# Another listed order up to the fourth tile, the first batch's evictions shared between ScalarE and VectorE, and spare transposes on TensorE, in an attention and two-MoE kernel on one core

## The chip, the core and the metric
The kernel runs on one core of a Trainium2 chip. The metric is the device time of one execution in microseconds (us), given as the median of several runs; a profiled execution comes with a trace. TensorE (PE) multiplies, and its weight loads are listed as PEld; VectorE is DVE, ScalarE is ACT, GpSimd is POOL, and SyncE (SP) issues the DMAs. Each engine works through its own list of instructions in order and waits for the others by semaphores.

## What is computed
```python
def sm_attn(qq, kk, vv):                      # softmax attention, scale 1/8
    s = scale * np.matmul(qq, kk.transpose(0, 1, 3, 2))
    a = np.exp(s - np.max(s, axis=-1, keepdims=True))
    a = a / (np.sum(a, axis=-1, keepdims=True) + 1e-09)
    return np.matmul(a, vv)
p_packed = sm_attn(p, k, v)                   # 8 batches, 8 heads, 576 tokens, 64 wide, 32 packs
x = sm_attn(q, p_packed, p_packed)            # as 4608 tokens x 512
h = x @ w_in                                  # 512 -> 1024
solu = h * softmax(h)
ln = layernorm(solu) * g_ln
y = ln @ w_out                                # 1024 -> 512
h2 = np.maximum(np.maximum(y @ w1, y @ w2), y @ w3)   # 512 -> 768
out = h2 @ w_out2                             # 768 -> 512
```
The weights arrive as float64 and are decoded to float32 on the chip.

## The kernel before, in words
Three stages follow each other. The first, about the first 520 us, computes for each of 36 tiles of 128 tokens the attention and the hidden row `h`, turns its normalised row (`u`) and multiplies it by `w_out` in groups of four tiles (`y`). The second is the maximum of three products (line 957), the third the last product (line 1235).

In the first stage each batch has two groups of four heads. `keys` (line 389) turns the packs (`tp` to `pT`) and the keys (`tp` to `kT`, four copies a group) through TensorE; `scores` multiplies them and VectorE takes the maxima (line 416); `powers` is the exponential on ACT (line 425, `e`); `weights` turns `e` into `e1T`; `values` multiplies by the values (`pv`), and two scalings give `ppz` (line 463 on ACT in batch 0, line 465 on VectorE in the others); `turned_values` turns that to `ppT`. `queries` turns the queries into `qT` (lines 644, 651 in batches 0 and 1). `product` multiplies the packed values by `w_in` (`mp`, line 485), and ACT copies it as `Mh` (line 490); `product_low` is the rest `Ml` on VectorE (line 496). `tokens` is the second attention's scores and exponential (lines 527 to 539, `st`, `x`), `shares` its normalisation and the pair `ah`, `al` (lines 548 to 566). `hidden_parts` gives `h` from three matmuls for each of two groups (`Mh` with `ah`, `Ml` with `ah`, `Mh` with `al`, line 686), for a tile in two halves, then a maximum on VectorE (line 694), an exponential on ACT (696), a product on VectorE (701), a square (707) and a scaling (722) on ACT. `y_transpose` (769 to 776) and `y_product` (798) follow, with the pair `lh`, `ll`.

`w_in` comes in eight pieces, each decoded in three steps: two operations on ACT (lines 128, 129), two on VectorE (132, 135), one on POOL (140). `w_out` is decoded likewise in four pieces for the left half and in small ones after that, and split into `woh` and `wol` (lines 213, 214).

The function `ev` (line 300) sends an eviction of PSUM to ACT ('s') or VectorE ('v'), as the table `CFG` says: the string of the key is read at a running number.

The order of the opening is written out in `CFG['st']`, one word a step. Up to the bar all five engines keep that order; behind the bar, and for all later tiles, a scheduler places the steps by its own estimate, also between the fixed ones. The words: `k`, `v`, `q` load keys, values, queries of a group; `L` loads a piece of `w_in`; `G` and `g` load and scale the gains; `K`, `s`, `e`, `i`, `E`, `p`, `t`, `Q` are keys, scores, powers, inverses, weights, values, turned values, queries; `x` and `a` are tokens and shares of a part of the batch; `n`, `m` the product and its low half; `1`, `2`, `3` the three steps of the next `w_in` piece; `o` loads a piece of `w_out`, `4` to `7` are the steps of its decode; `H0a` is the first half of tile 0, `H0b` its second, `H0x`, `H0c`, `H0d` what follows on the other engines; a `b` ahead of a word is batch 1.

Of the kernel before, what the change touches and what calls it, by code (L numbers as in the profile page):

```python
# [13 lines left out]
AF = mybir.ActivationFunctionType  # L14
# [5 lines left out]
def f32(ap):  # L20
# [5 lines left out]
    kT='s',  # L26
    qT='s',
    e1T='s',
    ppT='sv',
    pTz='s',  # L30
    yt='sv',
    look=3,
    s1='DFNTAHTDTyATyDyTAFy',
    s2='DFNTAHTTyTyDyTAFy',
    s3='DFNTAHTWTyTyyTWFy',
    t1=9,
# [1 line left out]
    nf=2,  # L38
    nb=1,
    st=(  # L40
# [3 lines left out]
    ),  # L44
    s0='TyTyFTyNFTyDFHD',
# [15 lines left out]
def kernel(  # L61
# [15 lines left out]
    nc = tc.nc  # L77
    B, H, S, D = q.shape
# [5 lines left out]
    P = 128  # L84
    KP = 96
    KJ = S // KP
    HALF = S // 2
    NPAIR = H // 2
# [16 lines left out]
    ident = const.tile([P, P], F32, name="ident")  # L105
# [85 lines left out]
    def decode_w_in(c, n):  # L191
        ns = slice(n * 512, (n + 1) * 512)
        src, i = words(w_in)[c * P:(c + 1) * P, ns, :], 4 * n + c - 6
        if i < 0:
            raw = wide(src)
        else:
            raw = early[0].bitcast(I32)[:, i * DFF:(i + 1) * DFF].rearrange("r (f t) -> r f t", t=2)
            nc.sync.dma_start(out=raw, in_=src)
        t = lt_p.tile([P, TB], F32, tag="ll", name="dt")
        return [*decode(w_in_sb[:, c, ns], raw, t, parts=True)]  # L200
# [95 lines left out]
    def ev(key, out, in_, n=0):  # L296
        e = CFG[key]
        e = e[n % len(e)]
        if e == 's':
            nc.scalar.copy(out, in_)  # L300
        elif e == 'v':
            nc.vector.tensor_copy(out, in_)

    def bank(name):
        return ps_t.tile([P, 512], F32, tag="t", name=name)
# [16 lines left out]
    qT, ppT, Mh, Ml, A = {}, {}, {}, {}, {}  # L322
# [7 lines left out]
    class Packed:  # L330
# [58 lines left out]

        def keys(self, g):  # L390

            tp = bank("tp")
            nc.tensor.transpose(tp[:, :P], self.p[:, g, :, :].rearrange("r a d -> r (a d)"), ident)
            ev('pTz', pT, tp[:, :P])
            kT = self.kT[g] = self.room_kT(g)
            for hh in range(4):
                tp = bank("tp")
                for jj in range(3):
                    nc.tensor.transpose(
                        tp[:, jj * KP:(jj + 1) * KP], self.kt[g][:, hh, jj * P:(jj + 1) * P], ident[:KP, :KP]  # L400
                    )
                ev('kT', kT[hh], tp[:, :HALF], hh)

        def scores(self, g):
            s1 = [bank("s1") for _ in range(2)]
# [42 lines left out]
        def values(self, g):  # L448
            b = self.b
            pv = bank("pv")  # L450
            for j in range(KJ):
                jj = 2 * (j % 3) + j // 3
                for hh in range(4):
                    nc.tensor.matmul(
                        pv[NP * hh:NP * (hh + 1), :D],
                        lhsT=self.e1T[g][j // 3][:, j % 3, NP * hh:NP * (hh + 1)],
                        rhs=self.vt[g][:, hh, jj * D:(jj + 1) * D],
                        start=(j == 0), stop=(j == KJ - 1),
                    )
            ppz = self.room_ppz(g)  # L460
            for r in range(2):
                if b == 0:
                    nc.scalar.activation(ppz[:, r, :], pv[:, :D], AF.Copy, scale=self.rim[g][:, r:r + 1])
                else:
                    nc.vector.tensor_scalar_mul(ppz[:, r, :], pv[:, :D], self.rim[g][:, r:r + 1])
            self.ppz[g] = ppz

        def turned_values(self, g):
# [32 lines left out]
        def queries(self, c):  # L501
            b = self.b
            if c == 0:
                qT[b] = qt_p.tile([P, NPAIR, S], F32, tag="qT", name="qT")
            full, rest = S // P, S % P

            def turn(out, j):
                nc.tensor.transpose(out, self.qt[c][:, j, :, :].rearrange("r h d -> r (h d)"), ident)

            for i in range(2):  # L510
                tp = bank("tp")
                for j in range(full):
                    turn(tp[:, j * P:(j + 1) * P], full * i + j)
                ev('qT', qT[b][:, 2 * c + i, :full * P], tp, i)
            tp = bank("tp")
            turn(tp[:, :P], 2 * full)
            ev('qT', qT[b][:, 2 * c:2 * c + 2, full * P:], tp[:, :P].rearrange("r (i t) -> r i t", i=2))
# [66 lines left out]
    class First(Packed):  # L584
# [51 lines left out]
        def queries(self, n):  # L636
            b = self.b
            if n == 0:
                qT[b] = qt_p.tile([P, NPAIR, S], F32, tag="qT", name="qT")
            for j in range(2 * n, 2 * n + 2):  # L640
                t0 = j * P
                tp = bank("tp")
                for i in range(NPAIR):
                    nc.tensor.transpose(
                        tp[:, i * P:(i + 1) * P], self.qt[j][:, 2 * i:2 * i + 2, :].rearrange("r h d -> r (h d)"), ident
                    )
                ev('qT', qT[b][:, :, t0:t0 + P], tp.rearrange("r (i t) -> r i t", i=NPAIR), j)
            if n == 1:
                tp = bank("tp")
                for c in range(2):  # L650
                    nc.tensor.transpose(
                        tp[:, c * P:(c + 1) * P], self.tail[:, c].rearrange("r h d -> r (h d)"), ident
                    )
                ev('qT', qT[b][:, :, S - S % P:], tp[:, :2 * P].rearrange("r (i t) -> r i t", i=NPAIR))

    def parts_of(t):

# [123 lines left out]
    def open_y():  # L781
        first_h.close()
        return late.enter_context(tc.tile_pool(name="ps_y", bufs=1, space=PSUM, reuse_waits="tile"))
# [247 lines left out]
    def load_w_out():  # L1031
        if left:
            n = left.pop(0)
            raw = u_p.tile([P, DFF], F32, tag="u", name="raw").bitcast(I32)
            src = words(w_out)[2 * n * P:2 * (n + 1) * P, :HM, :]
            nc.sync.dma_start(
                out=raw.rearrange("r (k c) -> r k c", k=2), in_=src.rearrange("(k r) f t -> r k (f t)", r=P)
            )
            raws.append((n, raw.rearrange("r (f t) -> r f t", t=2)))

    def start_step(w):
        nonlocal woh, wol
        if w == 'W':
            woh, wol = (big.tile([P, KFF, DM], F32R, tag=x, name=x) for x in ("woh", "wol"))
        elif w == 'L':
            for d, f in zip(dec_i, decode_w_in(*pieces.pop(0))):
                d.append(f)
        elif w in '123':
            dec_i[int(w) - 1].pop(0)()
        elif w == 'G':  # L1050
            nc.sync.dma_start(out=g_sb, in_=g_ln.rearrange("(c r) -> r c", r=P))
        elif w == 'g':
            nc.gpsimd.tensor_scalar_mul(g_sb, g_sb, 0.125)
        elif w == 'o':
            load_w_out()
        elif w == 'Y':
            rooms.append(open_y())
        elif w == 'T':
            step_t(0, KFF)
        elif w == 'y':  # L1060
            step_y(0, 2 * KFF)
        elif w in '4567':
            if w == '4':
                for d, f in zip(dec_o, decode_w_out(*raws.pop(0))):
                    d.append(f)
            dec_o[int(w) - 4].pop(0)()
        elif w[0] == 'H':
            t = int(w[1])
            if t not in parts:
                parts[t] = hidden_parts(t)  # L1070
            parts[t][w[2]]()
        elif w[0] == 'b':
            second.run(w[1:])
        else:
            first.run(w)
# [44 lines left out]
    def step_t(j, most):  # L1120
        n = turned.get(j, 0)
        if j >= 0 and n < min(most, KFF):
            y_transpose(j, n)
            turned[j] = n + 1

    with tc.manual_schedule(engines={ENGINES[e] for e in CFG['fix']}):
        for w in CFG['st'].split('|')[0].split():
            start_step(w)
    for w in CFG['st'].split('|')[1].split():
        start_step(w)  # L1130
# [10 lines left out]
    for t in range(4, nt):  # L1141
        j, i = t // 4 - 1, t % 4
# [61 lines left out]
    j = NB - 1  # L1204
# [140 lines left out]
```

## Time and profile before
| | |
|---|---|
| median of 3 runs | 1100.88 us (1099.74 to 1102.63) |
| profiled execution | 1099.66 us |
| its span | 1097.9 us |
| instructions in it | 17988 |
| TensorE busy | 1040.2 us, 95% |
| VectorE, ScalarE, GpSimd busy | 678.0, 504.8, 268.3 us |
| granted clock of TensorE, mean | 0.992 |

The span is the time from the first to the last instruction of the profiled execution; its own time adds what lies around it. Busy time counts an engine's instructions, and an engine that is not busy waits for another, for a DMA, or has nothing to do.

### The profile page before, as it was taken

Reading aid. Unit: us, or ns where it says so; the run is one execution under the profiler, and the core shown is the slowest. Engines: PE = TensorE matmul, PEld = TensorE weight load, DVE = VectorE, ACT = ScalarE, POOL = GpSimd, SP = SyncE. Lnnn points to the kernel's source line nnn. Section 1 sums busy time; section 2 is a strip of 40 time slices with the busy share of each in tenths; the row PEclk is TensorE's granted clock in tenths of the full one; section 3 lists DMA queues with packets and bytes.
Section 4 is the critical chain, followed back from the end, with each engine's and each line's share of the span. In section 5 each row is a group of like instructions: output and inputs, shape, how many; then the busy total and the mean of one; then the engine's idle time right before and its main releaser. Section 6 shows DMA issues by size and latency. Waiting matters only on the chain.

```text
span 1097.9 us, 17988 instructions
## 1 busy us (share of the span) xinstructions
PE 1040.2 (95%) x6548; PEld 874.3 (80%) x6548; DVE 678.0 (62%) x1318; ACT 504.8 (46%) x993; POOL 268.3 (24%) x293
## 2 busy tenths in 40 slices
PE   6668999999999999999999999999999999999997
PEld 4255767677675777777899999999989999999995
DVE  1858767777867685664898736725745663672560
ACT  4577867776786756566333421321231132132112
POOL 0413312121211200041576610320140042031002
PEclk9979999999999999999999999999999999999999
DMA  9723545556365623146564644444444453443411
GB/s 280 159 79 108 151 135 155 163 146 186 100 189 143 180 63 84 59 129 204 186 218 158 220 143 116 140 158 124 142 148 144 125 183 115 118 122 119 122 48 58
DMA packets 139463, 154.27 MB, mean 141 GB/s; under 512 B 51824, under 2 KB 92272, under 8 KB 139376
## 3 DMA queue, kind: packets, MB, share of 16 engines
q1 hardware_dynamic: 139376, 153.14, 47.6%
q8 instruction: 52, 0.85, 0.3%
q14 instruction: 35, 0.29, 0.1%
HBM read 116.92 MB, written 36.18 MB: 139 GB/s over the span
## 4 chain that ended last, share of the span: by engine, by line
PE 50%; DVE 2%; issue 1%; DMA 1%; POOL 1%; ACT 1%; DVEq 0%; ACTq 0%; POOLq 0%
PE m L957 32%; PE o L1235 12%; PE y L798 4%; PE h L686 1%; DVE wt L857 1%; DMA out_dram<-ob 1%; DVE r L965 0%; PE tp L769 0%; DVE kept L965 0%; POOL w2l L830 0%; DMA wt<-wodram 0%; DMA wt<-wdram 0%; ACT ob L1244 0%; ACT u L722 0%; POOL hl L1021 0%
## 5 line engine op out<-in xcount | busy, mean ns | idle before, releaser
L798 PE MATMUL y<-lh,woh 128*128 128x512 f32 x288 | 118.1, 416 | 0.6 <-ACT lh L775 0.6
L798 PE MATMUL y<-ll,woh 128*128 128x512 f32 x288 | 115.4, 401 | 0.0
L798 PE MATMUL y<-lh,wol 128*128 128x512 f32 x288 | 114.5, 398 | 0.0
L990 ACT COPY q<-m 128x384 f32<-128x384 f32 x54 | 25.9, 479 | 178.4 <-PE m L957 178.4
L965 DVE TENSOR_TENSOR u<-m,q 128x384 f32<-128x384 f32 x54 | 30.0, 555 | 125.0 <-PE m L957 65.2
L1021 POOL TENSOR_TENSOR hl<-cur,hh 128x384 fp32r<-128x384 f32 x36 | 40.5, 1128 | 235.8 <-ACT hh L1020 235.8
L140 POOL TENSOR_TENSOR wt<-raw 128x256 int32<-128x256 int32 (+1 forms) x60 | 40.4, 674 | 193.1 <-DVE raw L135 80.2
L1235 PE MATMUL o<-w2h,hh 128*128 128x512 f32 x216 | 84.3, 390 | 1.4 <-ACT ob L1244 1.4
L1235 PE MATMUL o<-w2h,hl 128*128 128x512 f32 x216 | 84.8, 393 | 0.6 <-POOL hl L1021 0.6
L1235 PE MATMUL o<-w2l,hh 128*128 128x512 f32 x216 | 84.5, 391 | 0.0
L686 PE MATMUL h<-Mh,ah 128*128 128x512 f32 x160 | 67.8, 424 | 7.6 <-DVE u L701 4.8
L686 PE MATMUL h<-Ml,ah 128*128 128x512 f32 x160 | 66.1, 413 | 3.1 <-DVE Ml L496 3.1
L686 PE MATMUL h<-Mh,al 128*128 128x512 f32 x160 | 65.4, 409 | 0.0
L798 PEld LDWEIGHTS y<-lh,woh 128*128 128x128 f32 x288 | 53.9, 189 | 14.1 <-issue 1.9
L798 PEld LDWEIGHTS y<-lh,wol 128*128 128x128 f32 x288 | 54.2, 188 | 12.8 <-issue 0.8
L957 PE MATMUL m<-b22h,s 128*128 128x384 f32 x216 | 63.7, 335 | 0.0
L798 PEld LDWEIGHTS y<-ll,woh 128*128 128x128 f32 x288 | 54.5, 189 | 11.5 <-DVE ll L776 0.7
L957 PE MATMUL m<-t1h,s 128*128 128x384 f32 x216 | 63.7, 335 | 0.0
L957 PE MATMUL m<-t2h,s 128*128 128x384 f32 x216 | 63.6, 335 | 0.0
L957 PE MATMUL m<-t3h,s 128*128 128x384 f32 x216 | 63.6, 335 | 0.0
L965 DVE TENSOR_TENSOR kept<-r,kept 128x384 f32<-128x384 f32 x72 | 59.3, 823 | 2.4
L776 DVE SCALAR_TENSOR_TENSOR ll<-tp,g_sb,lh 128x512 fp32r<-128x512 f32 x72 | 52.1, 743 | 14.0 <-ACT lh L775 13.8
(206 smaller groups left out, 2714.8 us busy)
## 6 DMA issues: line engine op xcount, KB each, us to landing
s<-sdram SPq DMA_DIRECT2D x188, 256.0 KB, 2.9
kt<-in_k_dram SPq DMA_DIRECT2D x16, 576.0 KB, 5.2
ydram<-yt SPq DMA_DIRECT2D x36, 256.0 KB, 2.9
raw<-in_moe_w_dram SPq DMA_DIRECT2D x36, 256.0 KB, 3.1
b<-ydram SPq DMA_DIRECT2D x24, 384.0 KB, 4.6
out_dram<-ob SPq DMA_DIRECT2D x36, 256.0 KB, 2.6
vt<-in_v_dram SPq DMA_DIRECT2D x14, 576.0 KB, 4.8
sdram<-s SPq DMA_DIRECT2D x28, 256.0 KB, 2.1
```

Of the source, the lines that this page charges most:

```text
L140: nc.gpsimd.tensor_tensor(out=dst.bitcast(I32), in0=hi, in1=lo, op=ALU.add)
L686: nc.tensor.matmul(at['h'][:, n, :], lhsT=x, rhs=m[:, g, n * 512:(n + 1) * 512], start=(i == 0), stop=(i == len(ops()) - 1),)
L776: last[nc.vector] = nc.vector.scalar_tensor_tensor(out=ll, in0=tp, scalar=gc, in1=f32(lh), op0=ALU.mult, op1=ALU.subtract)
L798: nc.tensor.matmul(ys[half][m], lhsT=w[:, kc, ms], rhs=x, start=(kc == 0 and i == 0), stop=(kc == KFF - 1 and i == 2),)
L857: nc.vector.tensor_tensor(out=out, in0=x, in1=y, op=op)
L957: nc.tensor.matmul(out, lhsT=w, rhs=y, start=start and i == 0, stop=i == len(ops) - 1, skip_group_check=not start,)
L965: mark[0] = nc.vector.tensor_tensor(**what)
L990: mark[1] = nc.scalar.copy(q, ba)
L1021: nc.gpsimd.tensor_tensor(out=hl, in0=t, in1=f32(hh), op=ALU.subtract)
L1235: nc.tensor.matmul(ops[i], lhsT=x[:, ts], rhs=w, start=(c == 0 and n == 0), stop=(c == KF2 - 1 and n == 2),)
```

## The change
Seven edits. (1) The order up to the bar of `st` is another: `e0` stands ahead of `s1`; `Q0` stands between the two value steps; five first steps of the `w_in` decode are listed around `t0 t1`, two full decodes ahead of `x0`; `H1a` is ahead of `x1`; `m1` is ahead of `a1`; batch 1's `K0` and `s0` are ahead of `H0x`. (2) `w` is a new word: twelve transposes of the identity into a spare bank that nobody reads. It stands twice ahead of `n0` and once behind `bs0`. (3) In batch 0 the key copies follow 'svsvvvvv' over both groups (two on ACT, six on VectorE) and the query copies 'vvsvs'; later batches keep ACT. (4) `pT` goes to VectorE in all batches. (5) `ppT` of batch 0 goes to VectorE. (6) `ppz` of batch 0 goes to VectorE. (7) Nothing is added or taken away but the 36 spare transposes; the lists behind the bar differ in places, since the scheduler places them anew.

```diff
-    ppT='sv',
-    pTz='s',
+    ppT='v',
+    kT0='svsvvvvv',
+    qT0='vvsvs',
+    pTz='v',
...
-        ... K0 s0 K1 s1 e0 i0 E0 e1 i1 E1 p0 t0 p1 t1 Q0 1 2 3 1 x0 2 3 1 1 2 3 2 3 1 ... 1 a0 2 3 n0 1 m0 H0a ...
+        ... K0 s0 K1 e0 s1 i0 E0 e1 i1 E1 p0 Q0 p1 1 t0 t1 1 1 1 2 3 2 3 1 x0 2 3 2 3 1 1 w w n0 a0 1 2 3 m0 H0a ...
-        'n1 W a1 m1 H0b H1b bq0 bq1 H0x g 5 6 H1x H0c H1c H0d H2a H2b ...
+        'n1 W m1 a1 H0b H1b bq0 bq1 bK0 bv0 g H0x H1x 5 6 bs0 w H0c H1c H2a H2b ...
...
-                ev('kT', kT[hh], tp[:, :HALF], hh)
+                ev('kT' if b else 'kT0', kT[hh], tp[:, :HALF], 4 * g + hh)
...
-                if b == 0:
-                    nc.scalar.activation(ppz[:, r, :], pv[:, :D], AF.Copy, scale=self.rim[g][:, r:r + 1])
-                else:
-                    nc.vector.tensor_scalar_mul(ppz[:, r, :], pv[:, :D], self.rim[g][:, r:r + 1])
+                nc.vector.tensor_scalar_mul(ppz[:, r, :], pv[:, :D], self.rim[g][:, r:r + 1])
...
-                ev('qT', qT[b][:, :, t0:t0 + P], tp.rearrange("r (i t) -> r i t", i=NPAIR), j)
+                ev('qT' if b else 'qT0', qT[b][:, :, t0:t0 + P], tp.rearrange("r (i t) -> r i t", i=NPAIR), j)
...
+        elif w == 'w':
+            tp = bank("warm")
+            for i in range(12):
+                nc.tensor.transpose(tp[:, i % 4 * P:(i % 4 + 1) * P], ident, ident)
```

The list of ACT in the opening, from the second group's exponentials (`e1`) to the first decode of `w_in` (`dt`, `raw`), before (the numbers are those of the buffers):
```order
L425 ACTIVATE e1_274,se1_276<-s1_240,m1_250 128x288
L425 ACTIVATE e1_275,se1_276<-s1_241,m1_250 128x288
L300 COPY e1T_284<-tp_286 96x384
L300 COPY e1T_285<-tp_291 96x384
L463 ACTIVATE ppz_321<-pv_296,rim_261 128x64 x2
L300 COPY ppT_324<-tp_325 128x128
L463 ACTIVATE ppz_353<-pv_328,rim_282 128x64 x2
L300 COPY ppT_324<-tp_356 128x128
L300 COPY qT_359<-tp_360 128x4x128
L300 COPY qT_359<-tp_366 128x4x128
L128 ACTIVATE dt_145<-raw_143 128x512
L129 ACTIVATE raw_143<-raw_143,ulps_73 128x512
```
and now:
```order
L428 ACTIVATE e1_274,se1_276<-s1_244,m1_254 128x288
L428 ACTIVATE e1_275,se1_276<-s1_245,m1_254 128x288
L302 COPY e1T_284<-tp_286 96x384
L302 COPY e1T_285<-tp_291 96x384
L130 ACTIVATE dt_145<-raw_143 128x512
L131 ACTIVATE raw_143<-raw_143,ulps_73 128x512
L130 ACTIVATE dt_148<-raw_146 128x512
L131 ACTIVATE raw_146<-raw_146,ulps_73 128x512
```
The scalings, `ppT` and `qT` that stood between `e1T` and the first decode on ACT are on VectorE's list now.

The list of VectorE from the second part's scores (`st`) over the soft-max of `x` to the first maxima of `h` (`nm`) and the decode behind it, before:
```order
L533 STREAM_TRANSPOSE x<-st 128x320 x2
L537 TENSOR_REDUCE mx_508<-x 128x20
L538 TENSOR_TENSOR x<-x,mx_508 128x640
L548 TENSOR_REDUCE sm_533<-x 128x20
L549 TENSOR_SCALAR sm_533<-sm_533 128x20
L550 RECIPROCAL sm_533<-sm_533 128x20
L551 TENSOR_TENSOR x<-x,sm_533 128x640
L564 STREAM_TRANSPOSE y<-x 128x320 x2
L496 SCALAR_TENSOR_TENSOR Ml<-mp,Mh 128x512 x2
L694 TENSOR_REDUCE nm<-h 128x1
L132 TENSOR_SCALAR dt<-dt 128x512
L135 SCALAR_TENSOR_TENSOR raw<-raw,dt 128x512
```
and now:
```order
L533 STREAM_TRANSPOSE x<-st 128x320 x2
L537 TENSOR_REDUCE mx_541<-x 128x20
L538 TENSOR_TENSOR x<-x,mx_541 128x640
L496 SCALAR_TENSOR_TENSOR Ml<-mp,Mh 128x512 x2
L548 TENSOR_REDUCE sm_561<-x 128x20
L549 TENSOR_SCALAR sm_561<-sm_561 128x20
L550 RECIPROCAL sm_561<-sm_561 128x20
L551 TENSOR_TENSOR x<-x,sm_561 128x640
L564 STREAM_TRANSPOSE y<-x 128x320 x2
L304 COPY pT<-tp 128x128
L694 TENSOR_REDUCE nm<-h 128x1 x2
L134 TENSOR_SCALAR dt<-dt 128x512
```
`Ml` moved ahead of the sum and what follows it, `pT` of batch 1 came in ahead of the first maximum, and the two maxima follow each other; batch 1's score maxima stand behind that decode now.

The list of ACT from the last scalings of tiles 2 and 3 (`u`) to the first `lh`, before:
```order
L300 COPY pT<-tp 128x128
L300 COPY kT<-tp 128x288 x4
L707 ACTIVATE spare,squares<-u,nmu 128x1024
L722 ACTIVATE u<-u,nmu,powers 128x1024 x2
L425 ACTIVATE e_707,se_708<-s_688,m_698 128x288
L425 ACTIVATE e_707,se_708<-s_689,m_698 128x288
L213 CAST woh<-wt 128x2x256
L300 COPY e1T<-tp 96x384 x2
L775 ACTIVATE lh<-tp,g_sb 128x512 x2
```
and now:
```order
L707 ACTIVATE spare,squares<-u,nmu 128x1024
L722 ACTIVATE u<-u,nmu,powers 128x1024 x2
L215 CAST woh<-wt 128x2x256
L775 ACTIVATE lh<-tp,g_sb 128x512 x2
L302 COPY kT<-tp 128x288 x2
L130 ACTIVATE dt<-raw 128x512
```
The copies of batch 1's first keys, its exponentials and `e1T` stand further ahead on ACT's list now.

## Rows read from the trace of the kernel before
**Rows 1.** The page: busy time by engine, and TensorE's busy tenths in 40 slices.
```profile
PE 1040.2 (95%) x6548; PEld 874.3 (80%) x6548; DVE 678.0 (62%) x1318; ACT 504.8 (46%) x993; POOL 268.3 (24%) x293
...
PE   6668999999999999999999999999999999999997
```
**Rows 2.** By stretch: length, PE, PEld, DVE, ACT, POOL busy (count), PEclk, DMA share, GB/s.
```profile
85.02:120.00 34.98, 30.91 (x316) 20.25 (x315) 28.76 (x64) 25.49 (x61) 16.60 (x18) 1.00 0.43 117
120.00:140.00 20.00, 20.00 (x202) 15.57 (x204) 12.75 (x37) 18.45 (x39) 3.31 (x5) 1.00 0.60 154
```
**Rows 3.** Timeline of the opening: start, busy time, engine, line, operation, [idle before <-releaser].
```profile
23.96 1.92 PE L644 MATMUL tp<-ident,qu 128*128 128x128 f32 x8
...
27.09 0.43 DVE L132 TENSOR_SCALAR dt<-dt 128x512 int32<-128x512 int32 x1 [8.47 <-ACT dt L128]
...
34.91 3.64 PE L485 MATMUL mp<-w_in_sb,ppT 64*32 64x512 f32 x8 [0.32 <-POOL w_in_sb L140]
...
35.54 1.04 POOL L140 TENSOR_TENSOR w_in_sb<-raw 128x512 int32<-128x512 int32 x1 [0.68 <-issue]
...
41.70 1.04 PE L644 MATMUL tp<-ident,qu 128*128 128x128 f32 x8
...
47.41 1.05 PE L485 MATMUL mp<-w_in_sb,ppT 64*32 64x512 f32 x4 [0.25 <-POOL w_in_sb L140]
```
**Rows 4.** Loads of `raw`: SP's issue, time to landing (nine, 0:60).
```profile
7.68 7.61 SPq L188 DMA_DIRECT2D raw<-in_moe_w_in_dram  x6
...
DMA to landing us min/median/max: 3.4/7.4/10.5
```
**Rows 5.** Timeline from the second part's scores to the first maximum of `h`.
```profile
46.11 0.90 DVE L533 STREAM_TRANSPOSE x<-st 128x320 f32<-128x320 f32 x2
...
48.81 0.74 ACT L539 ACTIVATE x<-x 128x640 f32<-128x640 f32 x1 [3.81 <-DVE x L538]
...
49.45 1.06 ACT L490 ACTIVATE Mh<-mp 128x512 fp32r<-128x512 f32 x2
...
52.72 1.25 DVE L496 SCALAR_TENSOR_TENSOR Ml<-mp,Mh 128x512 fp32r<-128x512 f32 x2
...
53.42 0.80 PE L686 MATMUL h<-Ml,ah 128*128 128x512 f32 x1 [2.83 <-DVE Ml L496]
...
55.96 1.22 DVE L694 TENSOR_REDUCE nm<-h 128x1 f32<-128x1024 f32 x1 [2.00 <-PE h L686]
```
**Rows 6.** Tiles 2 and 3: TensorE's stretch alone, their first matmul, their last maximum.
```profile
60.60:66.40 5.80, 5.74 (x14) 0.50 0.25 85
...
60.66 0.77 PE L686 MATMUL h<-Mh,ah 128*128 128x512 f32 x1 [3.13 <-DVE u L701]
...
69.19 1.23 DVE L694 TENSOR_REDUCE nm<-h 128x1 f32<-128x1024 f32 x1 [1.36 <-PE h L686]
```
**Rows 7.** By stretch as rows 2, then the first `lh` and batch 1's second scores.
```profile
57.28:81.65 24.37, 15.52 (x73) 11.64 (x72) 13.92 (x37) 19.55 (x36) 4.91 (x6) 0.76 0.29 88
...
81.65 0.69 ACT L775 ACTIVATE lh<-tp,g_sb 128x512 fp32r<-128x512 f32 x1 [0.38 <-PE tp L769]
...
85.02 0.93 PE L408 MATMUL s<-kT,pT 64*32 64x288 f32 x16
```
**Rows 8.** Copies by shape (busy, mean ns); TensorE's waits for `pT`, 130:620 (total, times, longest).
```profile
L302 DVE COPY yt<-y 128x512 f32<-128x512 f32 x18 | 12.4, 688 | 4.9 <-PE y L798 4.8
L302 DVE COPY ppT<-tp 128x128 f32<-128x128 f32 x14 | 4.0, 289 | 5.2 <-PE tp L473 5.2
L300 ACT COPY kT<-tp 128x288 f32<-128x288 f32 x24 | 8.5, 407 | 4.0 <-PE tp L399 3.8
L425 ACT ACTIVATE e<-s,m 128x288 f32<-128x288 f32 x10 | 4.9, 495 | 0.0
L300 ACT COPY e1T<-tp 96x384 f32<-96x384 f32 x10 | 4.7, 486 | 2.1 <-PE tp L443 2.1
...
PE tp L399 <- ACT pT L300: 4.2, 5, 1.2
```

More of the change, by code (lines that the diff above doesn't have):

```diff
@@ L390, in keys @@
         def keys(self, g):
+            b = self.b
             tp = bank("tp")
@@ L653, in queries @@
                     )
-                ev('qT', qT[b][:, :, S - S % P:], tp[:, :2 * P].rearrange("r (i t) -> r i t", i=NPAIR))
+                ev('qT' if b else 'qT0', qT[b][:, :, S - S % P:], tp[:, :2 * P].rearrange("r (i t) -> r i t", i=NPAIR), 4)
     def parts_of(t):
```

4 rows, old and new, of the table st are left out of this document.

## The prediction
> **What bounds the kernel now.** I read the page first, then the busy time by stretch, then the timeline of the stretches in which TensorE idles, last the waits. The page shows TensorE busy for 95% of the span, with weak slices only at the front [rows 1]. By stretch it never stops between 120 and 140 us, and still misses 4.1 us between 85 and 120 [rows 2]. The change lists another order for the part before that, so the question is how much sooner the unbroken stretch begins: what is saved ahead of it comes off the end, since behind it little but TensorE is waited for.
>
> Four places set that front part. (a) VectorE starts the second half of the first `w_in` decode at 27.09, after 8.47 us of waiting for ACT's `dt`, though the six loads were issued from 7.68 on and landed at most 10.5 us after their issue [rows 3, 4]; ahead of ACT's decode stand evictions, in queue order. The fourth piece leaves POOL at 35.54 + 1.04 = 36.58, and the product `mp` ends at 34.91 + 3.64 = 38.55 [rows 3]. (b) From x1's transposes at 46.11 VectorE runs the whole soft-max of x1 before `Ml`, which starts at 52.72; TensorE waits 2.83 us for it, and the first maximum of `h` starts at 55.96 [rows 5]. (c) The halves of tiles 2 and 3 start at 60.66 after 3.13 us without work, and run at half the granted clock: 14 matmuls in 5.74 us, 0.41 us each [rows 6]. (d) From the first exponential to the first `lh` (57.28 to 81.65) ACT is busy 19.55 of 24.37 us, part of it with batch 1's key copies and exponentials [rows 7].
>
> TensorE is at its lower level before 40 us too: the same eight transposes take 1.92 us at 23.96 and 1.04 us at 41.70, behind the product [rows 3].
>
> **The change part by part.** I add up the lead: how much earlier than before each milestone comes.
>
> *Evictions shared, decode earlier.* Six key copies, three query copies, the `ppz` scalings, `pT` and `ppT` leave ACT, so that its five decodes stand behind `e1T` alone and find their loads landed. A VectorE copy of 128x288 has no row; it lies between 0.29 us (128x128) and 0.69 us (128x512). I take 0.45, between them by columns; ACT's is 0.41 [rows 8]. The second group's `pT` now stands behind the maxima on VectorE, which I put at 0.5 us on the scores; the query transposes, now between the two value products, cover waits that I put at 1.1 us. VectorE, with the evictions, is free for the second halves about 0.6 us earlier by that, and another 0.6 since nothing waits for ACT: about 25.9, lead 1.2 on 27.09. From there to the end of the fourth piece VectorE and POOL have the work they had, 36.58 - 27.09 = 9.5 us, since x0's first steps stay inside it: 35.4.
>
> *Spares before the product.* 24 transposes at 0.24 us (1.92 / 8) or 0.13 us (1.04 / 8), 3.1 to 5.8 us, begin behind x0's scores near 27 and are over by 33; the fourth piece comes at 35.4, so they cost nothing. If they raise the clock the product ends 1.05 us behind its last piece, as the row at 47.41 does, not 38.55 - 36.58 = 1.97: end 36.4, lead 2.1 [rows 3].
>
> *To x1.* Behind the fourth decode VectorE has the work it had, plus one query copy of 0.69: x1's transposes at 46.11 - 1.2 + 0.7 = 45.6, its exponential over at 48.81 + 0.74 - 0.5 = 49.05 [rows 5, 8]. So the early decode is nearly eaten by here; VectorE is what holds the place.
>
> *`Ml` before the soft-max's second half.* Two `Mh` copies (1.06) follow the exponential, `Ml` (1.25) starts behind the first: 49.6 to 50.85. The second half (52.72 - 49.55 = 3.17) and one `pT` (0.29) follow: 54.3 [rows 5, 8]. The first maximum starts there against 55.96, lead 1.65, because `H0b` and `H1b` ran meanwhile. The next maximum follows at once, but a decode (about 1.1) and batch 1's score maxima (about 1.0) now stand ahead of `H0c`: `H2a` at about 60.2, lead only 0.4.
>
> *Keys of batch 1 and the third group of spares.* Thirteen transposes, eight scores, twelve spares and five transposes of `e` fill TensorE between `H1b` and `H2a`. The 24 matmuls of tiles 2 and 3 took 69.19 - 60.66 = 8.5 us, 14 of them low; the other ten 2.8, so 0.28 each with the tail [rows 6]. Should the clock stay up, 24 take between 24 x 0.205 = 4.9 (half the low pace) and 6.7; I take 5.7. All low they would be 9.8. The last maximum then starts near 66.0, lead 3.2.
>
> *ACT.* Between that maximum and `lh` lay 81.65 - 69.19 = 12.5 us. Of ACT's work in it four key copies, `pT`, two exponentials of `e` and one `e1T` are done earlier or elsewhere now: 4 x 0.41 + 0.3 + 2 x 0.5 + 0.5 = 3.4 [rows 8]. So 9.1 if all of it counts, 12.5 if none does; I take 10.4, nearer the lower since ACT hardly pauses there: first `lh` at 76.4, lead 5.2. From the other side: ACT's 19.55 us [rows 7] less 1.9 for key copies and `pT`, from 56.3 without a gap, ends at 74.0, lead 7.6.
>
> *Beyond.* From `lh` to batch 1's second scores (81.65 to 85.02) the work is alike [rows 7]; I take off 0.3 for a low clock: lead 4.9. Then the engines' lists read nearly as before. On SP the load of `p` for batch 2 moves ahead of the third and fourth piece of `w_out`; it waits for a transpose near 66, the third piece is wanted behind `lh` at 76.4, and a 512 KB load lands in 3.4 to 10.5 us [rows 4]: hidden, with little to spare. The 14 `pT` copies after the opening move to VectorE; TensorE waited 4.2 us in all for ACT's [rows 8]. I put the exchange at zero, from 4 gained to the last rival but one.
>
> **Sum.** 4.9 us off the profiled execution (1099.66, span 1097.9) gives 1094.8. The median of the three runs shown is 1.2 above it, so the time I give is 1096.0. A measurement here can tell about 0.3% from no change, 3.3 us: faster means under 1097.6.
>
> **The rivals.**
> *The spares do not count (0.18).* Transposes fill most of the first 28 us, and at 23.96 they still run at the low pace; it had doubled only behind the product [rows 3]. Then tiles 2 and 3 run as low as before, and their lead of 3.2 shrinks to the 0.4 of `H2a`: 1096.0 + 2.8 = 1098.8. Against it: the early transposes had gaps, these have none, and real products `H0b`, `H1b` run shortly before tiles 2 and 3. The Trainium skill (TensorE: Matmul & The Clock Gate, Part 4: PE-mode transpose) states that the full clock does not engage for transpose mode, since it does not count as busy in the same way. By that rule this rival is the outcome, 1098.8 and not 1096.0; the trace's first 28 us agree with it, but nowhere in it do transposes run alone without gaps.
>
> *The lead is lost behind 80 us (0.14).* ACT and VectorE are loaded there, 25.5 and 28.8 us of 35 [rows 2]; a `w_out` piece held back on SP, or `ll` behind another operation, would make TensorE wait. With 3 us lost: 1099.
>
> *Slower: `pT` on VectorE (0.07).* Ahead of a `pT` there can stand a maximum of 1.23 us [rows 6], and 14 times in batches 1 to 7 the key transposes or the scores wait for it. If each comes late by one such operation, 17 us; by half of one, 8.6: 1096.0 + 8.6 = 1104.6. It decides from about 0.6 us each, 8.2 in all, where the lead and the bound are used up. Against: TensorE has other matmuls listed between, and ACT was late too (the 4.2).
>
> *More than forecast (0.13).* ACT runs without gaps, as from the other side above: lead 7.6, 1093.3.
>
> **How the numbers follow.** The forecast (0.48, by itself 1094 to 1098) is the likeliest. The range reaches to the first two rivals and the larger lead, with a run's spread of 1.5 us on each side: 1091.5 to 1100.6. Faster: nine tenths of the forecast, all of the larger lead, a tenth of the two rivals of lost lead and some of what I name nowhere, 0.61. Slower by over 0.3% (above 1104.2): the `pT` rival, 0.07. Within: 0.32.
>
> **What would show it.** Right: VectorE's first second half near 26; `mp` over near 36.5; `Ml` ahead of the soft-max's sum, and the first maximum of `h` near 54.3; a granted clock of 1.00 while tiles 2 and 3 run, near 60 to 66; the first `lh` near 76.4; batch 1's second scores near 80; and from then on waits as before. Wrong: a clock near 0.5 between 60 and 66; `lh` near 80; TensorE waiting for `pT` for much over 4.2 us between 130 and 620.

## The result, and the profile after
The changed kernel takes 1090.29 us (median of five, 1088.36 to 1093.41), the kernel before on the same chip 1100.88 (1098.44 to 1102.63): a ratio of 0.9913, 95% interval 0.9886 to 0.9939. The medians stand 10.6 us apart; by the ratio it is 9.6. I had said 1096.0, 1091.5 to 1100.6: the direction was right, the gain about twice what I summed up. The profiled execution after took 1088.36 us (span 1086.4), the one before 1099.66 (span 1097.9).

The page of the changed kernel, busy times and TensorE's slices: the first three slices read 777 where they were 666 [rows 1], spares among what fills them.
```profile
PE 1038.7 (96%) x6584; PEld 875.2 (81%) x6584; DVE 686.5 (63%) x1349; ACT 495.6 (46%) x962; POOL 267.1 (25%) x293
...
PE   7778999999999999999999999999999999999997
```
The timeline of the changed kernel at the prediction's milestones (start, busy time, engine, line, operation):
```profile
25.54 0.42 DVE L134 TENSOR_SCALAR dt<-dt 128x512 int32<-128x512 int32 x1
...
26.24 2.84 PE L1055 MATMUL warm<-ident 128*128 128x128 f32 x24
...
34.72 1.87 PE L485 MATMUL mp<-w_in_sb,ppT 64*32 64x512 f32 x4 [0.67 <-POOL w_in_sb L142]
...
49.10 1.29 DVE L496 SCALAR_TENSOR_TENSOR Ml<-mp,Mh 128x512 fp32r<-128x512 f32 x2 [1.35 <-ACT Mh L490]
...
53.61 1.21 DVE L694 TENSOR_REDUCE nm<-h 128x1 f32<-128x1024 f32 x1
...
65.36 1.22 DVE L694 TENSOR_REDUCE nm<-h 128x1 f32<-128x1024 f32 x1 [1.13 <-PE h L686]
...
74.50 0.69 ACT L775 ACTIVATE lh<-tp,g_sb 128x512 fp32r<-128x512 f32 x1
...
78.20 0.73 PE L411 MATMUL s<-kT,pT 64*32 64x288 f32 x8
...
533.36 0.33 PE L957 MATMUL m<-b11h,a 128*128 128x384 f32 x1
```
The last row is the first product of the second stage; in the trace of the kernel before it stands at
```profile
542.16 0.33 PE L957 MATMUL m<-b11h,a 128*128 128x384 f32 x1
```
By stretch, the changed kernel (columns as in [rows 2]): first exponential to first `lh`, then tiles 2 and 3, then two stretches of the main part.
```profile
55.34:74.50 19.16, 13.87 (x77) 9.52 (x74) 13.73 (x38) 18.02 (x32) 4.39 (x7) 0.86 0.29 78
59.47:65.36 5.89, 5.89 (x28) 4.72 (x27) 3.62 (x15) 5.50 (x9) 0.00 (x0) 1.00 0.01 3
85.00:120.00 35.00, 30.21 (x260) 19.85 (x258) 28.34 (x61) 24.66 (x57) 14.94 (x17) 1.00 0.34 95
...
140.00:160.00 20.00, 17.67 (x121) 10.51 (x121) 15.31 (x33) 13.35 (x25) 2.90 (x6) 0.91 0.38 111
```
Read as a lead (the same instruction, before minus after): 27.09 - 25.54 = 1.6 at the decode; 52.72 - 49.10 = 3.6 at `Ml`; 55.96 - 53.61 = 2.4 at the first maximum; 69.19 - 65.36 = 3.8 at the last; 81.65 - 74.50 = 7.2 at `lh`; 85.02 - 78.20 = 6.8 at batch 1's second scores. The first stage ends 542.16 - 533.36 = 8.8 early, and the spans differ by 11.5. So 6.8 us are made in the opening, 2 between 85 and 540, and 2.7 behind that. ACT is busy 18.02 of 19.16 us from the first exponential to `lh`, where it was 19.55 of 24.37 [rows 7]; tiles 2 and 3 run at a granted clock of 1.00, not 0.50 [rows 6]. In 140:160 the clock is 0.91, where it was 1.00 before.

The waits of TensorE between 130 and 620 us in the changed kernel (total, times, longest): none for `pT`, which had 4.2 [rows 8], but
```profile
PE tp L473 <- DVE ppz L465: 3.7, 3, 2.0
PE tp L769 <- DVE x L533: 2.3, 1, 2.3
```
where before there stood
```profile
PE tp L473 <- DVE ppz L465: 1.8, 4, 0.8
```

### The profile page after: what moved, and what is told of

It reads as the page before. It is cut to its first block, busy times and chain, and to the rows that moved or that the text cites. A ratio compares the mean times of both kernels' runs of the same rounds, so it can differ in the third digit from the quotient of the medians.

```text
span 1086.4 us, 18066 instructions
## 1 busy us (share of the span) xinstructions
PE 1038.7 (96%) x6584; PEld 875.2 (81%) x6584; DVE 686.5 (63%) x1349; ACT 495.6 (46%) x962; POOL 267.1 (25%) x293
## 4 chain that ended last, share of the span: by engine, by line
PE 51%; DVE 2%; issue 1%; POOL 1%; DMA 1%; ACT 1%; DVEq 0%; ACTq 0%; POOLq 0%
PE m L957 33%; PE o L1239 13%; PE y L798 4%; PE h L686 1%; DVE wt L857 1%; PE tp L769 0%; DVE r L965 0%; POOL w2l L830 0%; DMA wt<-wodram 0%; DMA wt<-wdram 0%; ACT u L722 0%; DVE t L907 0%; DVE kept L965 0%; POOL hl L1021 0%; POOL t1l L925 0%
## 5 line engine op out<-in xcount | busy, mean ns | idle before, releaser
L990 ACT COPY q<-m 128x384 f32<-128x384 f32 x54 | 25.9, 479 | 177.2 <-PE m L957 177.2
L798 PEld LDWEIGHTS y<-lh,wol 128*128 128x128 f32 x288 | 54.1, 188 | 12.8 <-issue 0.8
L798 PEld LDWEIGHTS y<-ll,woh 128*128 128x128 f32 x288 | 54.4, 189 | 11.3 <-DVE ll L776 0.8
L776 DVE SCALAR_TENSOR_TENSOR ll<-tp,g_sb,lh 128x512 fp32r<-128x512 f32 x72 | 52.0, 743 | 14.1 <-ACT lh L775 13.9
```

Source lines behind the costliest of these rows:

```text
L776: last[nc.vector] = nc.vector.scalar_tensor_tensor(out=ll, in0=tp, scalar=gc, in1=f32(lh), op0=ALU.mult, op1=ALU.subtract)
L798: nc.tensor.matmul(ys[half][m], lhsT=w[:, kc, ms], rhs=x, start=(kc == 0 and i == 0), stop=(kc == KFF - 1 and i == 2),)
L990: mark[1] = nc.scalar.copy(q, ba)
```

## The experiments
I put two marks on each run: the lead over the kernel before at 126 us (the 44th `y` product, 125.53 before) and at the second stage's first product; and the clock that was lost between 120 and 540 us, (1 - granted clock) x 20 us, added up over 20-us stretches. Ratios are against the kernel before on the same chip.

| kernel | ratio (95%) | first `lh` | lead at 126 | lead at second stage | clock lost 120:540 |
|---|---|---|---|---|---|
| the change | 0.9913 (0.9886 to 0.9939) | 74.50 | 5.8 | 8.8 | 1.8 |
| the change again | 0.9917 (0.9890 to 0.9943) | 73.20 | 7.0 | 6.0 | 7.0 |
| `pT` back on ACT | 0.9919 (0.9899 to 0.9938) | 74.70 | 5.8 | 5.9 | 1.8 |
| all evictions on ACT | 0.9927 (0.9911 to 0.9943) | 74.76 | 5.7 | 5.8 | 1.8 |
| before, `pT` on VectorE | 0.9986 (0.9969 to 1.0004) | 81.36 | -0.4 | 2.6 | 1.8 |
| no spares | 0.9930 (0.9914 to 0.9946) | 76.62 | 2.9 | 7.5 | 0 |
| no spares again | 0.9944 (0.9924 to 0.9963) | 76.71 | 2.8 | 5.9 | 1.8 |
| no third group | 0.9934 (0.9911 to 0.9956) | 74.61 | 4.9 | 7.9 | 0 |
| no first groups | 0.9911 (0.9884 to 0.9937) | 75.43 | 4.8 | 8.7 | 1.8 |
| keys of batch 1 late | 0.9907 (0.9877 to 0.9938) | 77.63 | 2.5 | 6.2 | 1.8 |
| `m1` behind `a1` | 0.9919 (0.9894 to 0.9943) | 78.40 | 1.9 | 7.1 | 0 |
| before, 72 spares first | one execution, 1100.12 us | 80.93 | 0.9 | -2.5 | 3.4 |
| batch 4's `pT` on ACT | 0.9950 (0.9932 to 0.9969) | 76.82 | 3.4 | 2.3 | 5.2 |
| `pT` on VectorE in batch 4 | 0.9888 (0.9864 to 0.9912) | 71.14 | 9.4 | 14.1 | 0 |
| the same again | 0.9889 (0.9861 to 0.9916) | 74.70 | 6.0 | 10.1 | 0 |
| 12 late spares | 0.9926 (0.9904 to 0.9949) | 72.69 | 7.2 | 7.1 | 3.6 |

**The list alone, with every eviction on ACT (order0).**
```diff
-    ppT='v', kT0='svsvvvvv', qT0='vvsvs', pTz='v',
+    ppT='sv', kT0='s', qT0='s', pTz='ss',
```
with line 465's scaling on ACT in batch 0 again.

> The changed kernel's list with spares, all evictions on ACT as in the kernel before (pT too). Theory: the lead of the opening comes from the list (Ml first, batch 1's keys early), which the shared evictions only help by the 1.2 of the early decode: lead at batch 1's second scores 4 to 6, time 1095 to 1097. Rival, the evictions carry the opening, since ACT is what fills it: the first second half on VectorE later than 27, lead under 2, time over 1098.5.

Measured: 0.9927, 8.0 us less, more than the 3.9 to 5.9 that I expected (1095 to 1097 on 1100.9); the lead at 126 us is that of the change, 5.7 against 5.8. The list makes the opening. The shared evictions of batch 0 add nothing that shows: the first second half on VectorE comes at 24.99 here and at 25.54 in the change, though ACT's first decode starts at 24.30, not 19.93. The list was put back in two words alone (below); what its first half is worth, with `e0`, `Q0` and the decode steps ahead of `x0`, was not tried and stays open.

**`pT` on ACT again, and `pT` on VectorE alone (pt_back, pt_main).** From batch 1 on:
```diff
-    ev('pTz', pT, tp[:, :P])          # pTz='v' (change), 's' (before)
+    ev('pTz', pT, tp[:, :P], min(self.b, 1))   # pTz='vs', and 'sv'
```


> The changed kernel, with the copy of pT on ACT again from batch 1 on (batch 0 stays on VectorE). My theory: the opening gives some 7 us and pT on VectorE another 2.5 to 3, gained between 120 and 550 us. Then the lead at batch 1's second scores stays near 6.8, the wait of the key transposes for ACT's pT comes back (4 us in 130:620), and the time is near 1093. Rival, all of the gain is made in the opening and in the tail: the time stays at 1090.3, within 1.

> The kernel before, with nothing changed but pT on VectorE from batch 1 on. Theory: 2.5 to 3 us less than before, near 1098, with no lead at 80 us and some 3 at 560. Rival, the exchange is worth nothing by itself: 1101, within 1. Rival of the prediction, pT late behind maxima: 1105.

Measured: between 126 us and the second stage the kernel with `pT` back gains 0.1, that with `pT` alone moved gains 3.0, as the change does; the place is as expected. The times differ by less than they can tell: 0.9919 (1089.78) against the change's 0.9913 and 0.9917 (1090.29 and 1088.64), so the 1093 expected did not come; and the interval of `pT` alone, 0.9969 to 1.0004, reaches over no change. The trace of pt_back shows one wait doing much of the damage, with the fall of the clock behind it (0.63 us shown for a matmul that takes 0.39 at the upper pace):
```profile
234.38 0.67 PE L402 MATMUL tp<-ident,kt 96*128 96x96 f32 x3 [2.23 <-ACT pT L302]
...
236.55 0.63 PE L798 MATMUL y<-lh,woh 128*128 128x512 f32 x1
...
237.83 0.43 PE L686 MATMUL h<-Mh,ah 128*128 128x512 f32 x1
```

**Only batch 4 on ACT, only batch 4 on VectorE (pt_not4, pt_b4).**
```diff
+    ev('pTz' if self.b != 4 else 'e1T', pT, tp[:, :P])        # pt_not4
+    ev('pTz' if self.b in (0, 4) else 'e1T', pT, tp[:, :P])   # pt_b4
```


> The changed kernel with pT on ACT again in batch 4 alone. The kernels with pT on VectorE gained 3.0 to 4.9 us between 125 and 530 us, those with pT on ACT none (one lost 3), and the longest single wait for ACT's pT, 1.2 to 2.2 us, stands at batch 4's second group near 235. Theory, one place carries most of it: the lead at 530 us falls from 8.8 to 6 to 7, with a wait of 1 us or more for pT near 235. Rival, the gain is spread over all batches (four further waits of 0.4 to 0.7): lead 8 or more.

> The changed kernel with pT on ACT from batch 1 on, but on VectorE in batch 4. Theory, batch 4 carries most of it: lead at 530 us from 5.9 to 8 or more, although the waits for pT in batches 2, 5 and 7 stay. Rival, spread over all batches: 6.3 to 6.8. Rival, neither: the lists of the whole stage fall out differently with each kernel, and the gain has no place: lead unrelated to these, 3 to 6.

Measured: 2.3, far under the 6 to 7 expected, and 14.1, over the change's own 8.8. The kernels' lists agree up to 55 us, and still VectorE's first second half stands at 25.50 and 22.64, `Ml` at 50.54 and 45.98 and `lh` at 76.82 and 71.14; and the clock lost behind 120 us is 5.2 in one and 0 in the other. So I ran the change and pt_b4 again, side by side, with the kernel without spares.

> The changed kernel once more, beside two others on one chip. Kernels whose lists agree up to 60 us differ by up to 3.4 us at the first lh (71.1 to 76.8), and their granted clock in 40:120 stands for 5.2 to 10 us of lost time; in 120:540 it is 0, 1.8 or more. Theory, the clock falls at another place from one execution to the next: this profile has an lh more than 1 us from 74.5, or a fall at another place than 140:160, with the same lists. Rival, the same lists give the same falls: lh within 0.3 us of 74.5 and the fall at 140:160 again.

> The changed kernel with pT on VectorE in batches 0 and 4 alone, once more. Theory, its 14.2 us of lead at 530 us were the changed kernel's 8.8 and some 5 of luck with the clock (opening 2 to 3, main stage 1.8): within 2 us of the changed kernel beside it. Rival, it is the better division of work: again 4 us below the changed kernel.

The change again: `lh` at 73.20, and three falls of the clock instead of one,
```profile
140.00:160.00 20.00, 18.08 (x116) 9.77 (x115) 15.15 (x33) 12.15 (x23) 2.38 (x5) 0.83 0.31 94
300.00:320.00 20.00, 17.95 (x140) 13.96 (x139) 12.75 (x32) 12.67 (x26) 2.88 (x5) 0.91 0.58 162
360.00:380.00 20.00, 18.24 (x141) 14.39 (x140) 13.42 (x33) 13.00 (x26) 3.50 (x7) 0.91 0.58 160
```
so the same lists do not give the same falls. pt_b4 again has none, and is at 1084.90 against 1088.64 beside it; twice it was the fastest (0.9888, 0.9889), though the intervals overlap the change's. TensorE's waits in it, 130:620, show why it can be better: neither the long wait for `pT` nor the long ones for `ppz`.
```profile
PE tp L473 <- DVE ppz L465: 2.1, 4, 0.8
...
PE tp L402 <- ACT pT L302: 1.8, 3, 0.8
```
With `pT` on VectorE everywhere (and in pt_not4), `ppz` on that engine comes late instead: in all eleven such traces the longest wait for `ppz` between 120 and 500 us is 1.7 to 2.5 us, in the six others 0.8 to 1.3. This suggests moving the one batch whose `pT` is waited for longest, and leaving the rest on ACT. It is not shown: with the lost clock added back, pt_b4 gains 4.8 and 4.1 between the two marks, pt_not4 4.1, all within what the kernels with every `pT` moved gain (3.0 to 6.0, below). The timed runs say the same. Each has its mean granted clock on record; with (1 - clock) x time taken off each run, the means are 1077.0 and 1075.7 for the change and 1075.7 and 1076.4 for pt_b4. What sets pt_b4 apart is its clock, 0.991 against 0.987, and that its missing waits keep the clock up is likely, but argued.

**The spares (no_spares, no_third, no_first).** One, two or all three `w` taken out of the list.

> The changed kernel without all 36 spare transposes. Theory: TensorE had come up to its upper pace before the first spare, from work without gaps between 18 and 24.7, and keeps it or regains it by the products themselves; the spares are worth under 1 us: 1090.3 to 1091.3, tiles 2 and 3 at a pitch of 0.23. Rival, the third group of spares keeps the pace up: 14 of the 24 products of tiles 2 and 3 at 0.41, the last maximum some 2.8 later, 1093.

> The changed kernel without the third group of spares (the first 24 stay). Theory now: the third group alone is what the spares are worth: the products of tiles 2 and 3 start at half pace again, 7 or so at 0.43 us each, the last maximum comes near 67.5 (65.4 in the changed kernel), the lead at 530 us falls from 8.8 to about 7.4, time 1.3 more than the changed kernel's. Rival, the first 24 do the work: the last maximum stays at 65.4 and so does the lead.

> The changed kernel without the first 24 spares (the third group stays). Theory: TensorE waits for the decode there anyway, and the pace comes up in that stretch by other work, or not, from one execution to the next; last maximum within 0.7 of 65.4, lead at 530 us 8.3 to 9.3, time unchanged. Rival, the first groups are worth the other part of what is lost without all spares (7.3 there, 8.0 without the third group): lead near 7.9.

> The changed kernel without spares, once more. Theory, the spares ahead of tiles 2 and 3 are worth 1 to 2 us by the clock there (half pace again near 60 us), time 1 to 2 us over the changed kernel beside it. Rival, that too was luck: upper pace from 60 us on, time within 0.5 us.

Measured: my first theory of tiles 2 and 3 fell, though no_spares' 1091.27 lies within the time that it gave. Without the third group tiles 2 and 3 begin at half pace in all three executions, with it in none of the others with the new list. In no_spares_again, the first product and the stretch:
```profile
60.49 0.78 PE L686 MATMUL h<-Mh,ah 128*128 128x512 f32 x1
...
60.40:67.70 7.30, 7.30 (x28) 5.87 (x28) 3.57 (x13) 5.47 (x9) 0.00 (x0) 0.79 0.00 0
```
28 matmuls took 5.89 us in the change's stretch above, so some 1.4 are lost here, and `lh` comes 2.1 and 2.2 later than 74.50. The timed runs put all spares at 1.4 to 3.4 us (0.9930 and 0.9944 against 0.9913 and 0.9917), with intervals that overlap. The first 24 show no worth (0.9911 without them); they stand where TensorE waits for the decode. no_third's `lh` at 74.61 is not against this: in that execution the pace had come up by 18 us, and in the change only at 24 to 25. The same six transposes of `e`, in no_third:
```profile
17.99 1.01 PE L446 MATMUL tp<-ident,e 128*96 128x128 f32 x6 [1.06 <-ACT e L428]
```
and in the change:
```profile
18.00 1.52 PE L446 MATMUL tp<-ident,e 128*96 128x128 f32 x6 [1.05 <-ACT e L428]
```
So no_third's `Ml` started at 47.10, 2.0 us sooner; the last maximum still came at 65.63, no sooner than the change's 65.36. The half pace of [rows 6] is partly chance as well: pt_main and warm_first, with the old list and no spares there, begin tiles 2 and 3 at the upper pace (0.47 us for the first matmul, not 0.77) and stand at a granted clock of 0.77 over them.

**Two words of the list put back (undo_keys, undo_m1).**
```diff
-... bK0 bv0 g H0x H1x 5 6 bs0 w ... H2c 4 H3c H2d H3d |
+... g H0x H1x 5 6 w ... H2c 4 bK0 bv0 H3c H2d bs0 H3d |     # undo_keys
-n1 W m1 a1
+n1 W a1 m1                                                  # undo_m1
```


> The changed kernel with batch 1's first keys and scores back where they were, behind H2c and H2d. Theory: half of the opening comes from them, since they move ACT's key copies ahead of the exponentials: the stretch from the last maximum to the first lh grows from 9.1 to about 12 us, lh near 77.5, lead at 530 us near 6, time 3 more than the changed kernel's. Rival, ACT has room there: lh within 1 us of 74.5, time unchanged.

> The changed kernel with m1 behind a1 again, so that VectorE ends the soft-max of x1 before Ml. Theory: the first maximum of h goes from 53.6 to about 55.5 to 56 and the rest follows it: lh near 76.5, lead at 530 us near 7, time 2 more than the changed kernel's. Rival, the next wait (ACT, or the decode on VectorE) sets lh: the first maximum is late and lh is not, time unchanged.

Measured: in the traces both go the way expected, undo_m1 further than that. undo_keys has its last maximum at 64.80 and its `lh` at
```profile
77.63 0.69 ACT L775 ACTIVATE lh<-tp,g_sb 128x512 fp32r<-128x512 f32 x1 [0.38 <-PE tp L769]
```
12.8 us apart, not 9.1; undo_m1 has its first maximum at 57.59 (55.5 to 56 expected) and `lh` at 78.40 (76.5). At 126 us they are 3.3 and 3.9 behind the change; at the second stage 2.6 and 1.7, and 1.8 of what undo_m1 catches up is the fall of the clock that the change had there and undo_m1 had not. The timed runs don't show the 3 and 2 us that I expected: 0.9907 and 0.9919. So the two words are shown in the traces' openings, one execution each, and not in the time; what the 8.0 us of the list divide into stays open.

**Do transposes bring the pace up? (warm_first)** Six `w` ahead of `K0` in the kernel before:
```diff
-... q1 G K0 s0
+... q1 G w w w w w w K0 s0
```


> The kernel before with 72 spare transposes of the identity ahead of all other work of TensorE, one behind the other. They delay the opening; only their own pace is asked for. Theory (transposes bring the pace up as other matmuls do): they begin at 0.24 us each and go to 0.12 to 0.13 before the last. Rival (by the Trainium skill, TensorE: Matmul & The Clock Gate, Part 4, transposes do not bring the full clock): all 72 at 0.24, 17 us.

Measured, two stretches of the 72 transposes and the product behind them:
```profile
2.72 2.55 PE L1055 MATMUL warm<-ident 128*128 128x128 f32 x11
...
6.75 2.46 PE L1055 MATMUL warm<-ident 128*128 128x128 f32 x21
...
28.84 1.05 PE L485 MATMUL mp<-w_in_sb,ppT 64*32 64x512 f32 x4 [2.38 <-POOL w_in_sb L140]
```
and the same first piece of the product in the kernel before:
```profile
29.58 1.92 PE L485 MATMUL mp<-w_in_sb,ppT 64*32 64x512 f32 x4 [1.93 <-POOL w_in_sb L140]
```
The transposes take 0.23 us each at first, 0.12 later, with nothing but transposes on TensorE; the piece of the product takes 1.05 us where it took 1.92. The level doubles (1.2 to 2.4 GHz) on transposes alone. By the Trainium skill (TensorE: Matmul & The Clock Gate, Part 4: PE-mode transpose) the full clock does not engage for transpose mode. This run shows that it does here, for float32 transposes by a matmul with the identity; whether they run in the mode that the page means, the trace does not tell. The opening gained 0.9 us by 126 although its first scores began 4.2 us late (12.97 against 8.77).

**A try at more (late0):** no first groups, 12 spares behind tile 3.

> A try at a better version: the changed kernel without the first 24 spares and with 12 more behind the last product of tile 3, in the gaps of TensorE between 65 and 68. In the changed kernel the pace falls there from 68.9 to 79.8, where scores, transposes and y take some 4 us more than at the upper pace. If the spares hold it up, lead at y's 9th step and at 530 us 1 to 2 us more than the changed kernel's. Rival: what follows waits for ACT and VectorE, and nothing is gained; or the spares delay tile 4 by 1 us.

Measured: 0.9926, no gain; lead 7.2 at 126 (the change again, 7.0), none of it gained on to the second stage, with 3.6 us of clock lost on the way.

## Why the prediction was right and wrong
*Right, place by place.* The decode on VectorE was at 25.54 (I said 25.9), `mp` over at 34.72 + 1.87 = 36.6 (36.4), `Ml` at 49.1 (49.6), the first maximum at 53.6 (54.3), the last at 65.4 (66.0) with the clock at 1.00. The rival "the spares do not count" fell, and so did the reason I gave for half of my doubt: warm_first shows that transposes raise the pace (and in the trace before they fill 11.2 of the first 28 us, not most of them). The rival "slower by `pT`" has a cousin in the trace (`ppz`, not `pT`, late on VectorE, 3.7 us), but not its size. "The lead is lost behind 80 us" came true for 1.0, from 6.8 at 78 us to 5.8 at 126. "More than forecast" (0.13) is what the opening did: ACT nearly without gaps, and a lead of 7.2 at `lh` against that rival's 7.6; its 1093.3 lacked the terms 2 and 3 below. (Its 56.3 for the first exponential has no row: 54.3 and the 1.32 us from maximum to exponential before [rows 5, 7] give 55.6; it came at 55.34.)

*Right by luck.* The early decode was put down to the shared evictions; with all of them on ACT it comes at 24.99, so it is the list's. The end of the product is right by two errors that cancel: the last piece came by 34.7, not 35.4, and its four matmuls took 1.87 us, not 1.05. Nor did the spares bring the pace up ahead of it. Without them the first piece of the product runs at the upper pace too, in no_spares:
```profile
27.21 1.05 PE L485 MATMUL mp<-w_in_sb,ppT 64*32 64x512 f32 x4 [1.71 <-POOL w_in_sb L142]
```

*Wrong: three terms.*
1. "I take 10.4, nearer the lower", between the last maximum and `lh`. It is 74.50 - 65.36 = 9.1, the end at which all of ACT's moved work counts. ACT was the bound there, and the trace before could have told: the stretch from the last maximum to `lh`, before,
```profile
69.19:81.65 12.46, 6.75 (x47) 4.88 (x46) 7.20 (x21) 11.82 (x25) 3.88 (x5) 0.80 0.43 130
```
and in the change:
```profile
65.36:74.50 9.14, 4.99 (x22) 2.87 (x20) 6.11 (x16) 9.08 (x15) 2.61 (x4) 0.70 0.36 97
```
ACT is busy 11.82 of 12.46 us, then 9.08 of 9.14, and the 3.4 us taken from it came off in full. It is no chance of one execution: the thirteen with the early keys have 9.0 to 9.2 us there, the four with the late ones (undo_keys among them) 12.5 to 13.2. With 0.6 by the last maximum this makes the opening 6.8, not 4.9.
2. "I put the exchange at zero", the `pT` copies from batch 1 on. The lead grew by 3.0 between 126 us and the second stage, in the change as in pt_main, and by 0.1 in the two kernels that have the new list and `pT` on ACT. With the lost clock added back, the ten executions with `pT` on VectorE everywhere gain 3.0 to 6.0 there over the kernel before, the three others with it on ACT 0 to 1.9. The wait went, 4.2 us for `pT`; half came back as a wait for `ppz`; and both can bring the clock down. By the timed runs as they stand the exchange is worth 0.2 to 1.5 us, within their uncertainty. With (1 - clock) x time taken off each run, the change's 1077.0 and 1075.7 stand against 1079.4 with `pT` back and 1079.1 with all evictions on ACT: some 3 us again, most of which the change loses to its lower clock (0.987 against 0.990 and 0.989).
3. "4.9 us off the profiled execution" took the lead as final at 80 us. Behind the first stage it grew by 0.8 at the first products and by 1.7 at the last stores. The kernel before, the third `ob` and the product that waits for its bank:
```profile
1081.14 0.69 ACT L1244 ACTIVATE ob<-o,z 128x512 f32<-128x512 f32 x1 [2.98 <-DMA out_dram<-ob]
...
1081.88 0.50 PE L1235 MATMUL o<-w2h,hh 128*128 128x512 f32 x1 [1.39 <-ACT ob L1244]
```
The changed kernel, the same `ob`:
```profile
1069.70 0.69 ACT L1248 ACTIVATE ob<-o,z 128x512 f32<-128x512 f32 x1 [1.11 <-DMA out_dram<-ob]
```
One store took 3.9 us to land before (4.3 in pt_main), none over 2.1 in the change. Every other kernel but pt_main gained 1.0 to 1.5 us between the first and the last of the third stage's products, and all but pt_main and the two without spares the 0.8, warm_first with the old list too; so neither is the new order's, and they may be the one profiled execution's of the kernel before. What they are was not tried and stays open.

Together: 5.8 at 126 us, 3.0 to the second stage, 0.8, 1.7: 11.3, the difference of the two profiled executions. The timed runs give the list 8.0, where the prediction had 4.9 for list, evictions and spares together, and everything else 1.1 to 1.5, inside the intervals.

My range was too narrow for a reason of its own: kernels with the same lists differ by several microseconds by where the clock falls, and I had allowed 1.5. (Its ends, by its own numbers, are 1091.8 and 1100.5, not 1091.5 and 1100.6.)

## What to carry to other kernels
Where an engine is busy over nine tenths of a stretch that another waits for, take every moved instruction off it in full. After moving an eviction from one engine to the other, ask batch by batch which wait is longest on either side, and try moving only the copies that are waited for; two executions here suggest it, and do not prove it. A few spare transposes in a gap of TensorE can hold its pace for real work behind it; where the next thing waited for a decode they did nothing here. And a term of 1 or 2 us can be read from the traces of several executions, with the clock taken into account, but not from one.

## What I had not expected of the hardware
The granted clock falls in the middle of a kernel that keeps TensorE busy for 96% of the time. Each of the 15 falls between 120 and 540 us in these traces stands behind a single wait of 1.7 to 2.7 us (2.33 for `x` at 147.0 in the change, 2.23 for `pT` in pt_back), and costs 1.8 us as a rule, up to 3.4. But not each such wait brings one: the kernel before waits 2.17 us for `x` at 152.7 and no_spares 2.00 for `ppz` at 309.9, both at a clock of 1.00 in their stretches, and no_third even 2.52. In one kernel, two executions lost 1.8 and 7.0 us so. And in the opening the pace came up before 18 us in four executions with the new list and at 22 to 25 in the other ten, with TensorE's list the same up to there.
